# The order of the key-block segments in the value products of a sliding-window attention kernel

## The chip, the cores and the metric

The kernel runs on one core of a Trainium2 chip. The metric is the device time of one execution, in microseconds (us); smaller is better.

## The reference

A layer norm feeds two branches, and their sum is added to the input: a causal attention with a window of 256 tokens (2048 tokens, 32 heads of 16), and a bilinear gated projection.

```python
def _A_ref(x, wqkv, wo):                       # attention; H = 32, Dh = 16, W = 256
    qkv = ...; q, k, v = qkv[0], qkv[1], qkv[2]
    scores = jnp.einsum("bhqd,bhkd->bhqk", q, k) * (Dh ** -0.5)
    mask = (idx[:, None] - idx[None, :] >= 0) & (idx[:, None] - idx[None, :] < W)
    p = _softmax(jnp.where(mask[None, None], scores, -1e9), axis=-1)
    o = jnp.einsum("bhqk,bhkd->bhqd", p, v)    # <- the value products
    return o.transpose(...).reshape(B, S, D) @ wo
def _B_ref(x, w_gate, w_up, w_down):           # (x @ w_gate) * (x @ w_up) @ w_down
    ...
xn = _layernorm(A_x)
return A_x + _A_ref(xn, ...) + _B_ref(xn, ...)
```

## The kernel before

The kernel plans the order of all work itself and keeps TensorE fed with dense products (128 x 128 weights, mostly 512 columns) between the pieces of attention. The tokens are cut into 4 chunks of 512, the heads into 4 sets of 8, which gives 16 value products, here called groups. One group multiplies, for 8 heads at once, the attention strips `P` (keys on the partitions, queries along the columns) with `V`.

A **segment** is one block of 64 keys with the queries that see it: `(k, q, m, at)` is key block `k`, first query block `q`, `m` query blocks (1 to 5) of 64 columns each, and the place `at` in its strip. The first chunk has 9 segments, the others 12:

```python
def layout(T):
    if T == 0:
        return [[(2, 2, 4, 0), (4, 4, 4, 4)], [(0, 0, 5, 0), (5, 5, 3, 5)],
                [(1, 1, 5, 0), (6, 6, 2, 5), (7, 7, 1, 7)], [(3, 3, 5, 0), (2, 6, 1, 5)]]
    return [[(3, 3, 5, 0), (-3, 0, 2, 5), (-4, 0, 1, 7)], [(2, 2, 5, 0), (6, 6, 2, 5), (7, 7, 1, 7)],
            [(0, 0, 5, 0), (5, 5, 3, 5)], [(1, 1, 5, 0), (-2, 0, 3, 5)], [(-1, 0, 4, 0), (4, 4, 4, 4)]]
```

The group takes its segments longest first. Each is 8 matmuls on 8 tiles of the array (2 lanes of 64 rows, 4 strips of 32 columns, of which 17 are used), each with a weight load (LDWEIGHTS) of its own. All segments add into the same two banks, so any order gives the same result but for rounding:

```python
def i_values(self, T, c, strips, banks):
    segments = sorted(((P, s) for P, batch in strips for s in batch), key=lambda x: -x[1][2])
    for n, (P, (k, q, m, at)) in enumerate(segments):
        U, j = divmod(8 * T + k, 8)
        for lane in range(2):
            rows = slice(64 * lane, 64 * lane + 64)
            for e in range(4):
                self.nc.tensor.matmul(
                    banks[lane][32 * e:32 * e + 17, 64 * q:64 * (q + m)],
                    lhsT=self.V[U % 3][rows, j, 4 * c + e, 0:17],
                    rhs=P[rows, e, 64 * at:64 * (at + m)],
                    start=n == 0, stop=n == len(segments) - 1, ...)
```

By length, in blocks, the order is 5,5,5,5,4,4,3,3,2,2,1,1, and 5,5,5,4,4,3,2,1,1 in the first chunk. A group of 12 segments has 96 matmuls ("96-group"; there are 12), one of 9 has 72 ("72-group"; there are 4).

The softmax here doesn't subtract the row's maximum and nothing guards it: scores larger than these inputs give would overflow.

## Time and profile before

| | before |
|---|---|
| time, median of 5 runs | 268.03 us (267.75 to 268.22) |
| PE busy | 260.2 of 265.6 us |
| value products in the chain of waits | 7.4% |
| a 96-group (11 of the 12) / a 72-group, first start to the start of the next product | 1.302 us / 1.047 us |

The head of the page of the kernel before: the span, then busy time and share of each engine. PE is matmul, PEld weight loads.

```profile
span 265.6 us, 7999 instructions
PE 260.2 (98%) x3458; PEld 131.9 (50%) x3458; DVE 189.5 (71%) x365; ACT 165.5 (62%) x122; POOL 119.8 (45%) x272
PEclk9999999999999999999999999999999999999999
```

The two groups of instructions of the value products in the same page: line, engine, operation, tiles, shapes, count, then busy us and mean ns of one, then idle time of the engine just before them.

```profile
L236 PE MATMUL M<-P,V 64*17 64x320 bf16 (+4 forms) x1440 | 20.9, 252 | 0.0
L236 PEld LDWEIGHTS <-V 64*17 64x17 bf16 x1440 | 17.7, 86 | 3.5 <-issue 1.3
```

The chain of waits of the kernel before, in its shares by engine and by line (the view cuts its second line off), and then parts of it in order of time (start us, us, what): a 72-group, and one 96-group between its neighbours.

```profile
PE 95%; DMA 2%; DVE 1%; ACT 0%; issue 0%; DVEq 0%
by line: PE M L204 71.8%; PE S L212 9.4%; PE M L236 7.4%; PE M L664 5.7%; DMA x<-in_A_x_dram 0.9%; DMA out_dram<-xn 0.6%; PE S L204 0.6%; DVE xn L757 0.5%; PE M L603 0.5%; DVE st L577 0.3%; ACT xnT L198 0.2%; issue 0.2%; DVE xn L264 0.2%; A
```

```profile
34.84 1.04 PE M L236 x72
...
112.87 0.65 PE M L204 x3
113.52 0.33 PE S L212 x12
113.85 1.30 PE M L236 x96
115.15 0.01 issue
115.16 1.89 PE M L204 x8
```

PE is the chain. The value products (L236) stand in it with their whole length, no wait of PE stands in front of them, and what they lose or gain shifts everything after. But "busy" hides what goes on inside: PE counts as busy in a group even while it starves (1.30 us busy of the 1.30 us from 113.85 to 115.15 us). The single starts in the trace show that. This is the 96-group that begins at 113.78 us, times in ns from its first start (first and eighth matmul of each segment, first and eighth weight load; worked out from the instruction records):

```
segment blocks   loads         matmuls start   to the next segment
   1      5       -2 ..   21      0 ..   23     141
   2      5       25 ..   48    141 ..  165     136
   ...
   7      3      660 ..  683    767 ..  790      83
   8      3      769 ..  792    850 ..  873      82
   9      2      851 ..  899    932 ..  955      56
  10      2      934 .. 1008    988 .. 1012      56
  11      1     1016 .. 1090   1044 .. 1095      75
  12      1     1099 .. 1173   1119 .. 1177       -
next product                   1301 to 1304 in 11 of the 12 groups, 1375 in this one
```

In this trace a segment of 5, 4, 3 and 2 blocks takes 136, 109, 82.5 and 56 ns to the next one, about 26.7 ns a block; carried on, one of one block should take 29 ns (an estimate from these four). At the end it doesn't: the loads, 3.3 ns apart until then, come 8.3 ns apart from the fourth load of segment 9 on, the first one-block segment takes 75 ns, and the matmuls of the last straggle over 58 ns in place of 23. In this one group the next product really starts 73 ns later than in the others, at 1375 ns: two instructions that only wait for semaphores stand in front of it in the records (at 1157 and 1268 ns), then comes its first load (1344 ns). The chain above shows these 73 ns not as a wait but in the length of the next piece, 1.89 us, since a piece is counted from the end of the one before it.

### The profile page before, as it was taken

How to read it: one execution, taken by the hardware profiler on the slowest of the kernel's cores; microseconds unless marked ns; L12 is line 12 of the kernel's file. 1: busy time of each engine (PE TensorE's matmuls, PEld its weight loads, DVE VectorE, ACT ScalarE, POOL GpSimd, SP SyncE). 2: the span in 40 equal slices, each digit the busy share in tenths (PEclk: the TensorE clock that was granted, in tenths of full speed). 3: DMA queues.
4: the chain of work that ended last, by engine and by line, in shares of the span. 5: the costliest groups of instructions: out<-in, count | busy, mean ns of one | idle time of the engine just before them, and what ended most of it. 6: DMA issues, size and time to landing. Idle time of an engine off the chain costs nothing.

```text
span 265.6 us, 7999 instructions
## 1 busy us (share of the span) xinstructions
PE 260.2 (98%) x3458; PEld 131.9 (50%) x3458; DVE 189.5 (71%) x365; ACT 165.5 (62%) x122; POOL 119.8 (45%) x272
## 2 busy tenths in 40 slices
PE   7999999999999999999999999999999999999994
PEld 6974443654445344464534354456545354544562
DVE  4889987888996629687996629796754449787404
ACT  3637675677677666777667676567886766673000
POOL 1404664554356463708256454718064545537000
PEclk9999999999999999999999999999999999999999
DMA  6999920000001300000001400000000000000002
GB/s 187 373 373 351 225 42 0 4 2 0 4 2 32 89 22 23 0 2 2 2 0 44 81 22 20 0 6 0 2 2 22 21 22 22 0 2 0 2 2 80
DMA packets 17251, 13.88 MB, mean 52 GB/s; under 512 B 7104, under 2 KB 17216, under 8 KB 17216
## 3 DMA queue, kind: packets, MB, share of 16 engines
q1 hardware_dynamic: 16848, 13.11, 17.0%
q8 instruction: 27, 0.44, 0.8%
q10 hardware_dynamic: 368, 0.26, 0.4%
q14 instruction: 8, 0.07, 0.1%
HBM read 9.70 MB, written 2.10 MB: 44 GB/s over the span
## 4 chain that ended last, share of the span: by engine, by line
PE 95%; DMA 2%; DVE 1%; ACT 0%; issue 0%; DVEq 0%
PE M L204 72%; PE S L212 9%; PE M L236 7%; PE M L664 6%; DMA x<-in_A_x_dram 1%; DMA out_dram<-xn 1%; PE S L204 1%; DVE xn L757 1%; PE M L603 0%; DVE st L577 0%; ACT xnT L198 0%; DVE xn L264 0%; ACT ve L581 0%; DVE mv L578 0%; DVE rs L584 0%
## 5 line engine op out<-in xcount | busy, mean ns | idle before, releaser
L488 ACT ACTIVATE P<-S 128x2048 bf16<-128x2048 f32 x76 | 140.9, 1854 | 55.6 <-PE S L212 52.3
L221 POOL TENSOR_SCALAR_AFFINE_SELECT P<-P 64x256 bf16<-64x256 bf16 (+1 forms) x248 | 112.6, 456 | 117.6 <-ACT P L488 104.9
L204 PE MATMUL M<-xnT,Wg 128*128 128x512 bf16 x224 | 57.7, 380 | 0.0
L204 PE MATMUL M<-xnT,Wu 128*128 128x512 bf16 x224 | 57.7, 380 | 0.0
L204 PE MATMUL M<-Wd,hT 128*128 128x512 bf16 (+1 forms) x224 | 52.1, 373 | 0.0
L715 DVE TENSOR_TENSOR hT<-M,gsb 128x512 bf16<-128x512 f32 x56 | 38.2, 682 | 7.7 <-PE M L204 7.4
L204 PEld LDWEIGHTS <-hT 128*128 128x128 bf16 x238 | 21.7, 98 | 23.5 <-issue 2.1
L204 PEld LDWEIGHTS <-Wu 128*128 128x128 bf16 x224 | 20.5, 98 | 25.1 <-issue 2.3
L204 PEld LDWEIGHTS <-Wg 128*128 128x128 bf16 x224 | 20.1, 98 | 24.5 <-issue 2.8
L200 DVE CAST gsb<-M 128x512 bf16<-128x512 f32 x40 | 27.5, 686 | 5.3 <-PE M L204 5.0
L524 DVE STREAM_TRANSPOSE at<-M 128x512 f32<-128x512 f32 x32 | 21.4, 699 | 12.5 <-PE M L236 12.5
L204 PE MATMUL M<-xnT,Wqkv 128*128 128x128 bf16 (+1 forms) x224 | 30.3, 288 | 0.0
L212 PE MATMUL S<-Q,K 32*128 32x320 bf16 (+3 forms) x720 | 30.0, 254 | 0.0
L227 DVE TENSOR_TENSOR P<-P,masks 128x512 int16<-128x512 int16 x56 | 22.7, 412 | 9.2 <-ACT P L488 9.2
L212 PEld LDWEIGHTS <-K 32*128 32x128 bf16 x720 | 11.9, 92 | 32.3 <-issue 31.3
L275 DVE TENSOR_SCALAR K<-M,own 128x512 bf16<-128x512 f32 x28 | 20.0, 742 | 3.4 <-PE M L204 3.2
L204 PEld LDWEIGHTS <-Wqkv 128*128 128x128 bf16 x224 | 15.8, 98 | 10.7 <-issue 1.2
L236 PE MATMUL M<-P,V 64*17 64x320 bf16 (+4 forms) x1440 | 20.9, 252 | 0.0
L236 PEld LDWEIGHTS <-V 64*17 64x17 bf16 x1440 | 17.7, 86 | 3.5 <-issue 1.3
L757 DVE TENSOR_TENSOR y<-M,x 128x512 bf16<-128x512 f32 x12 | 8.2, 682 | 14.8 <-PE M L204 14.8
L204 PE MATMUL M<-Wo,OT 128*128 128x512 bf16 (+1 forms) x64 | 16.2, 374 | 0.0
L664 PE MATMUL M<-Wqkv,xnT 128*64 128x256 bf16 x256 | 15.7, 274 | 0.3 <-ACT xnT L198 0.3
(51 smaller groups left out, 134.1 us busy)
## 6 DMA issues: line engine op xcount, KB each, us to landing
Wg<-in_B_w_gate_dram SPq DMA_DIRECT2D x2, 896.0 KB, 10.1
Wu<-in_B_w_up_dram SPq DMA_DIRECT2D x2, 896.0 KB, 12.1
Wqkv<-in_A_wqkv_dram SPq DMA_DIRECT2D x3, 512.0 KB, 5.4
out_dram<-y SPq DMA_DIRECT2D x12, 128.0 KB, 1.7
x<-in_A_x_dram SPq DMA_DIRECT2D x1, 1024.0 KB, 13.9
Wd<-in_B_w_down_dram SPq DMA_DIRECT2D x2, 512.0 KB, 11.9
Wd<-in_B_w_down_dram SPq DMA_DIRECT2D x2, 384.0 KB, 8.5
x<-in_A_x_dram SPq DMA_DIRECT2D x1, 512.0 KB, 11.4
```

The lines of the kernel that those rows point to most:

```text
L200: self.nc.vector.tensor_copy(out=out, in_=in_)
L204: self.nc.tensor.matmul(ps, lhsT=a, rhs=b, start=first and n == 0, stop=last and n == len(pairs) - 1)
L212: self.nc.tensor.matmul(self.S[:, e, 64 * at:64 * (at + m)], lhsT=self.K[U % 3][rows, c, j].rearrange("p l t -> p (l t)"), rhs=self.Q[T % ...
L221: self.nc.gpsimd.affine_select(out=v, in_=v, pattern=[[0, 4], [0, n], [sign, 64]], base=0, fill=0.0, compare_op=ALU.is_gt if kind else ALU ...
L227: self.nc.vector.tensor_tensor(out=v, in0=v, in1=m, op=ALU.bitwise_and)
L236: self.nc.tensor.matmul(banks[lane][32 * e:32 * e + 17, 64 * q:64 * (q + m)], lhsT=self.V[U % 3][rows, j, 4 * c + e, 0:17], rhs=P[rows, e, ...
L275: self.nc.vector.tensor_scalar(out=out, in0=in_, scalar1=own, scalar2=None, op0=ALU.mult)
L488: ex = self.op(f"exp{g}", {"A": (took + 0.06, took + 0.18)}, [o], lambda e: self.nc.scalar.activation(out=P[:, :, 0:hi], in_=self.S[:, :, ...
L524: t = self.op(f"tr{v}", {"V": (0.63, 0.71)}, [o] + ts, lambda e, par=par: nc.vector.transpose(out=self.at[:, :, par, :], in_=self.M[banks[ ...
L664: self.nc.tensor.matmul(self.M[i][64 * lane:64 * lane + 64, 256 * jj:256 * jj + 256], lhsT=self.xnT[T % 2][:, k, tok], rhs=w[:, lane], sta ...
L715: x = self.op(f"u{T}.{f}", {"V": PSUM_COPY["V"]}, [o, ("gate", T, f)], lambda e: self.nc.vector.tensor_tensor(out=self.hT[T % 2][:, f, :], ...
L757: self.nc.vector.tensor_tensor(out=keep["y"][:, cols], in0=self.M[i][:, cols], in1=self.x[:, t, cols], op=ALU.add)
```

## The change

The intent, from the reading of the end of this group: a short segment gives the next one's weight loads no time to hide, so no two short ones should stand together. Nothing else changes.

```diff
     def i_values(self, T, c, strips, banks):
-        segments = sorted(((P, s) for P, batch in strips for s in batch), key=lambda x: -x[1][2])
+        rest = sorted(((P, s) for P, batch in strips for s in batch), key=lambda x: -x[1][2])
+        segments = []
+        while rest:
+            segments.append(rest.pop(0))
+            if rest:
+                segments.append(rest.pop())
         for n, (P, (k, q, m, at)) in enumerate(segments):
```

The new orders are 5,1,5,1,5,2,5,2,4,3,4,3 and 5,1,5,1,5,2,4,3,4.

## The prediction

> **What bounds the kernel.** TensorE. The page shows PE busy 260.2 of 265.6 us (98%), granted clock full. The chain of waits puts 95% of the span on PE, and 7.4% (19.7 us) on the value products (L236) that the change reorders. There are 16 groups of them, all in the chain, with no wait of PE in front of any: four of 72 matmuls (first chunk, 1.04 us each) and twelve of 96 (1.30 us each). What a group loses or gains is therefore lost or gained by the kernel.
>
> **Inside a group** (starts of single matmuls and weight loads in the trace, group at 113.8 us). A segment is 8 matmuls on 8 tiles of the array, starting 3.3 ns apart. From one segment to the next it takes 136, 109, 82.5 and 56 ns for 5, 4, 3 and 2 blocks of 64 columns[...]; a one-block segment should take 29 ns. But at the end, where the short ones stand together (3,3,2,2,1,1), weight loads no longer come at 3.3 ns: from the third-last segment on they arrive one per 8.3 ns with a gap of 24, about 82.5 ns for 8. The first one-block segment takes 75 ns, and the last one's matmuls straggle over 58 ns in place of 23. The loads for a segment are issued only when the segment before it starts, so a short segment hides few of them. By streaming alone the last start of the 96-group would come at 1068+23 = 1091 ns; it comes at 1177: 86 ns lost. In the 72-group it is 794+23 = 817 against 928: 111 ns lost. After the last start 98 ns plus its columns pass until the next product starts.
>
> **What the change does.** Same 1440 matmuls, same loads, same columns; only the order: 5,1,5,1,5,2,5,2,4,3,4,3 and 5,1,5,1,5,2,4,3,4. The loads behind each short segment then have a long one to hide in. Nothing is added on another engine. A pair 5,1 streams in 165 ns and needs 2 x 82.5 = 165 ns of loads at the starved rate: it just keeps up, and the later pairs (192 ns) have room. The groups should take (estimates from the sums above) 1302 -> about 1220 ns and 1046 -> about 945 ns. Full gain 12 x 0.082 + 4 x 0.10 = 1.4 us. If the starved rate holds already in the early pairs, some 35 to 50 ns of straggling stay in each group, and the gain is about 0.6 us. The strips of the last batch are needed later than before, so no new wait for a mask or an exponential; ACT (62%) and DVE (71%) follow PE.
>
> **Predicted.** 266.9 us, 8 in 10 between 266.3 and 267.9: a gain of about 0.45%. Faster by over 2%: 0.01; within 2%: 0.98; slower by over 2%: 0.01.
>
> **What would show it right.** PE M L236 in the chain falls from 7.4% to about 6.9%; a 96-group takes about 1.22 us to the next product and a 72-group about 0.95; one-block segments take near 29 ns (short of 40); the last segment's matmuls start 3.3 ns apart; all other pieces of the chain keep their lengths.
>
> **What would make it wrong.** Weight loads that can't follow a one-block segment even behind a long one (instruction supply too slow: straggling just moves); a stall when a short product accumulates onto columns just written; a PE wait for a mask newly exposed, since several groups start 50 to 65 ns after a write of an attention strip; or the shifted schedule meeting a PSUM bank not yet free.

No term of the forecast's sum goes with it: the 136, 109, 82.5 and 56 ns are measured, the 29 ns are the estimate above from these four, the streaming sum of the 96-group is 4 x 136 + 2 x 109 + 2 x 82.5 + 2 x 56 + 29 = 1068 ns to its last segment, and the full gain stays 12 x 0.082 + 4 x 0.10 = 1.4 us. That loads are issued with the start of the segment before is read from the table above (first load of segment 8 at 769 ns, first matmul of segment 7 at 767; 851 and 850 for the next).

## The result, and the profile after

The changed kernel takes 267.11 us, median of 5 runs (266.87 to 267.79), against 268.03 us. The ratio is 0.9969, 95% interval 0.9954 to 0.9985. Ratios here and below are the mean time of one kernel's fast runs over that of the other's of the same rounds, so not quite the ratio of the medians quoted. It is the same within 2%, and a little faster, clear of the noise.

The same lines of the page after the change (the line numbers moved by 5).

```profile
span 264.9 us, 7986 instructions
PE 260.4 (98%) x3458; PEld 131.0 (49%) x3458; DVE 190.1 (72%) x365; ACT 165.4 (62%) x122; POOL 119.2 (45%) x272
```

```profile
L241 PE MATMUL M<-P,V 64*17 64x320 bf16 (+4 forms) x1440 | 20.2, 252 | 0.0
...
L241 PEld LDWEIGHTS <-V 64*17 64x17 bf16 x1440 | 15.8, 85 | 2.8 <-issue 1.3
```

The chain of waits after the change, its shares by engine and by line, then the same stretches of it in order of time, and the last group.

```profile
PE 97%; DMA 1%; DVE 1%; ACT 0%; issue 0%
by line: PE M L204 72.0%; PE S L212 9.4%; PE M L241 7.2%; PE M L669 5.7%; PE M L194 1.8%; DMA out_dram<-xn 0.6%; PE S L204 0.6%; DVE xn L762 0.5%; PE M L608 0.5%; ACT xnT L198 0.2%; issue 0.1%
```

```profile
34.93 0.97 PE M L241 x72
...
113.26 0.33 PE S L212 x12
113.59 1.27 PE M L241 x88
114.86 1.83 PE M L204 x8
...
245.99 1.25 PE M L241 x96
```

The matmuls of the group are busy 20.2 in place of 20.9 us, and the 96-group takes 1.27 in place of 1.30 us. (The chain says x88 presumably because some matmuls start out of the program's order: in this group the eighth of segment 6 starts at 548 ns, and three of segment 7 at 528 to 540 ns. All 96 are there.) The piece behind it, 1.83 in place of 1.89 us, no longer holds the 73 ns by which the next product was late before: the same two waiting instructions now come at 997 and 1108 ns, and the product starts at 1270. Over the 16 groups, from the first start to the next product's and without those 73 ns: before 4 x 1.047 + 12 x 1.302 = 19.81 us, after 4 x 0.976 + 11 x 1.270 + 1.249 = 19.12 us, 0.69 us less. From the first start of the first group to the end of the span, the profile falls by 0.77 us (230.85 to 230.08): these 0.69 us and the 73 ns. The spans as a whole differ by 0.7 us, since the first group starts 0.09 us later after the change (34.86 against 34.77 us), and the first 5 us of the two chains run over different work (before, over the load of `x`; after, over the matmuls of L194 that keep TensorE busy at the start). So the gain is all in the value products and in the one product behind them, and that of the groups is half of the 1.4 us that the prediction called the full gain.

Inside the group after the change (the one that begins at 113.52 us; same columns as before):

```
segment blocks   loads         matmuls start
   1      5       -2 ..   22      0 ..   23
   2      1       25 ..   48    142 ..  165
   3      5      143 ..  167    170 ..  193
   4      1      172 ..  195    307 ..  330
   5      5      308, 333, 342 .. 383   335, 339, 346 .. 379, 413
   6      2      418 ..  476    472 ..  548
   ...
  12      3      930 .. 1014   1020, 1025, 1033 .. 1066, 1095
next product                   1270
```

The first half is what the change wanted: the one-block segments take 28 and 28 ns (142 to 170, 307 to 335), not 75. But from segment 5 on the loads come 8.3 ns apart, *behind a short one and behind a long one alike*, and the straggle runs on to the last segment, 75 ns from first to eighth start. One group, the last, ends better: its last segment straggles over 54 ns and it takes 1.249 us.

### The profile page after: what moved, and what is told of

It reads as the page before. It is cut to its first block, busy times and chain, and to the rows that moved or that the text cites. A ratio compares the mean times of both kernels' runs of the same rounds, so it can differ in the third digit from the quotient of the medians.

```text
span 264.9 us, 7986 instructions
## 1 busy us (share of the span) xinstructions
PE 260.4 (98%) x3458; PEld 131.0 (49%) x3458; DVE 190.1 (72%) x365; ACT 165.4 (62%) x122; POOL 119.2 (45%) x272
## 4 chain that ended last, share of the span: by engine, by line
PE 97%; DMA 1%; DVE 1%; ACT 0%; issue 0%
PE M L204 72%; PE S L212 9%; PE M L241 7%; PE M L669 6%; PE M L194 2%; DMA out_dram<-xn 1%; PE S L204 1%; DVE xn L762 1%; PE M L608 0%; ACT xnT L198 0%
## 5 line engine op out<-in xcount | busy, mean ns | idle before, releaser
L221 POOL TENSOR_SCALAR_AFFINE_SELECT P<-P 64x256 bf16<-64x256 bf16 (+1 forms) x248 | 112.2, 455 | 117.4 <-ACT P L493 105.1
L241 PE MATMUL M<-P,V 64*17 64x320 bf16 (+4 forms) x1440 | 20.2, 252 | 0.0
L241 PEld LDWEIGHTS <-V 64*17 64x17 bf16 x1440 | 15.8, 85 | 2.8 <-issue 1.3
```

The costliest lines, as they stand in the source:

```text
L221: self.nc.gpsimd.affine_select(out=v, in_=v, pattern=[[0, 4], [0, n], [sign, 64]], base=0, fill=0.0, compare_op=ALU.is_gt if kind else ALU ...
L241: self.nc.tensor.matmul(banks[lane][32 * e:32 * e + 17, 64 * q:64 * (q + m)], lhsT=self.V[U % 3][rows, j, 4 * c + e, 0:17], rhs=P[rows, e, ...
```

## The experiments

### Two theories

The **neighbour theory** is the prediction's and the change's: the loads of a segment start when the segment before it starts, and hide behind that one. A short one with long neighbours is well placed.

The **queue theory** is the author's reading of the two traces. They show no queue; the word is a picture for what the starts show. In the change the loads of the first 32 pairs of load and matmul, four segments, keep up with the matmuls, and the loads fall behind from the second load of segment 5, pair 34. Suppose that the supply reaches 32 pairs ahead and goes on only when the oldest matmul has *completed*, in program order; then the load of pair p+33 waits for the completion of pair p's matmul. The starts say so, with one constant (completion is start plus duration in the records):

```
kernel   matmul of pair p completes           load of pair p+33 starts                between
after    1st of segment 1:    0 + 302 =  302   2nd load of segment 5:   333            31
before   1st of segment 6:  658 + 269 =  927   2nd load of segment 10:  958            31
before   1st of segment 7:  767 + 243 = 1010   2nd load of segment 11: 1040            30
before   1st of segment 8:  850 + 243 = 1093   2nd load of segment 12: 1123            30
```

(The first load of each of these segments, that of pair p+32, is let in already: it starts early, at 308, 934, 1016 and 1099 ns.) After that the supply gives one pair per 8.3 ns. A long matmul holds its place longer: 302 ns for the first five-block one, 189 ns for a one-block one. By this reading segment k+4 has all its loads in time only if four segments in a row, k to k+3, stream for at least the duration of segment k's matmul plus about 60 ns (31 + 6 x 8.3 + 4 from load to matmul, less the 23 ns by which the eighth start trails anyway). In the change, 5,1,5,1 stream for 136 + 29 + 136 + 29 = 330 ns and would need 302 + 60 = 362.

I worked out the starts of any order from these rules (an estimate from numbers of the two traces: a reach of 32 pairs, 27 ns from a completion to the first instruction let in, which is the 31 ns to the late load less half of 8.3, 8.3 ns a pair, 3.3 ns a pair where the loads keep up, 136, 109, 82.5, 56 and 29 ns a segment of 5 to 1 blocks on each tile, 98 ns plus the last segment's columns, 27 ns a block, to the next product). For the kernel before they give 1.299 us a 96-group, measured 1.302, and 0.998 us a 72-group, measured 1.047; that last difference is told below (two semaphore updates, with which it is about 1.048). Each kernel below is the changed kernel, or where it is said the kernel before, with only the order, or what the diff shows, altered.

### The changed kernel again

No edit; it is timed here on the chip of the next three.

> The changed kernel again, on the same chip as the three other orders. Both theories: groups of 96 take 1.27 us to the next product (1.25 for the last), groups of 72 take 0.976 us; time about 0.7 to 0.8 us under the kernel before (ratio about 0.997).

Measured: correct; 267.09 us against 268.09 us before, ratio 0.9964 (0.9950 to 0.9977). The groups are as before: 1.270 us, and 0.975 to 0.976 us. This repeats the result on another occasion.

### Short one first

```diff
-            segments.append(rest.pop(0))
+            segments.append(rest.pop())
             if rest:
-                segments.append(rest.pop())
+                segments.append(rest.pop(0))
```

> Order 1,5,1,5,2,5,2,5,3,4,3,4 (and 1,5,1,5,2,5,3,4,4): alternation as in the change, but the short one first. Neighbour theory (a segment's loads hide behind the one segment before it; each short one still stands between long ones): as the change, 1.27 and 0.976 us a group. Queue theory [...]: the first segment's matmuls complete after 189 ns in place of 302, so supply for segment 5 resumes early: 1.22 to 1.24 us for a 96-group, 0.945 for a 72-group; 0.4 to 0.5 us faster than the change, ratio to before about 0.995.

Measured: correct; 266.78 us, ratio 0.9951 (0.9935 to 0.9966). Its chain of waits has this for a 96-group:

```profile
113.97 0.33 PE S L212 x12
114.30 1.24 PE M L241 x96
```

1.243 us, 3 ns over the expected range, and 0.949 us for a 72-group. But for the first and the last segment the neighbours are those of the change, so the neighbour theory has no reason for a difference; the queue theory has one, and its size: with a one-block segment in front the first matmul completes at 195 ns, not 302 (the second load of segment 5 starts at 226 ns in place of 333).

### Windows of four that last long enough

```diff
-        while rest:
-            segments.append(rest.pop(0))
-            if rest:
-                segments.append(rest.pop())
+        for m in (5, 3, 3, 5, 1, 4, 5, 1, 5, 4, 2, 2) if T else (4, 5, 1, 3, 5, 2, 4, 5, 1):
+            segments.append(next(x for x in rest if x[1][2] == m))
+            rest.remove(segments[-1])
```

> Order 5,3,3,5,1,4,5,1,5,4,2,2 (and 4,5,1,3,5,2,4,5,1), found with the queue theory so that any four segments in a row last long enough. It ends with two short ones together. Queue theory: no straggle at all, last segment's starts 3.3 ns apart, 1.22 us and 0.943 us a group, ratio to before about 0.9945. Neighbour theory: the closing 2,2 pays about 26 ns and the last one straggles 35 ns, 1.28 us, no better than the change.

Measured: correct; 266.59 us (266.27 to 267.09), ratio 0.9945 (0.9931 to 0.9958), the fastest correct kernel. Its chain and its line in the page:

```profile
113.41 0.33 PE S L212 x12
113.75 1.22 PE M L240 x96
```

```profile
L240 PE MATMUL M<-P,V 64*17 64x320 bf16 (+4 forms) x1440 | 19.5, 252 | 0.0
```

1.218 us a 96-group (1.23 the first; in the third the next product, the one that was late before, comes 48 ns late again) and 0.944 us a 72-group, against 1.22 and 0.943 expected. The last segments start at 991 .. 1014 and 1047 .. 1070 ns: no straggle, with two short ones together at the very end. The sum of the groups is 4 x 0.944 + 12 x 1.218 = 18.39 us, 1.42 us under before. So the full gain that was predicted for the change exists; it takes another order.

### Short ones together, windows as in the change

The edit is as in the last, with the orders 5,5,1,1,5,5,2,2,4,4,3,3 and 5,5,1,1,5,2,4,3,4.

> Order 5,5,1,1,5,5,2,2,4,4,3,3 (and 5,5,1,1,5,2,4,3,4): short ones stand together again, but not at the end. Neighbour theory: each 1,1 costs about 53 ns and the 2,2 about 26 more than in the change, so 1.30 us or more for a 96-group, no gain over before. Queue theory: sums over four segments are those of the change, so 1.25 to 1.275 us and 0.98 us, the same as the change; the two one-block segments run in 29 ns each.

Measured: correct; 267.42 us, ratio 0.9972 (0.9959 to 0.9986). Its chain:

```profile
114.10 1.27 PE M L240 x92
```

96-groups take 1.270 us, as in the change (in one of them the last start is 22 ns later), and 72-groups 0.986 us. The two one-block segments that stand together start at 278, 306 and the next at 335: 28 and 29 ns each. Standing together costs a short segment nothing there; the straggle comes at segment 5, as in the change, whose first four segments have the same sum. The neighbour theory falls.

### Alternating, but late

The orders are 5,5,5,5,3,1,3,1,4,2,4,2 and 5,5,5,3,1,4,1,4,2.

> Order 5,5,5,5,3,1,3,1,4,2,4,2 (and 5,5,5,3,1,4,1,4,2): no two short ones stand together, as the change wants it, but the four longest go first. Neighbour theory: as the change or nearly, 1.27 and 0.98 us a group, ratio about 0.997. Queue theory: the windows of four segments from 3,1,3,1 on are too short (about 225 ns against 243 ns for a three-block matmul to complete, plus the refill), so the loads straggle as before: 1.30 to 1.31 us and about 1.00 to 1.02 us a group, ratio about 0.999 to 1.000.

Measured: correct; 267.55 us, ratio 0.9981 (0.9967 to 0.9996). Its chain:

```profile
113.45 0.33 PE S L212 x12
113.78 1.30 PE M L240 x91
```

1.303 us and 1.003 us. No two short ones stand together, and the 96-groups gain nothing at all over the kernel before. The alternation is thus not what helped.

### Short ones together at the start

```diff
-        segments = sorted(..., key=lambda x: -x[1][2])        (the kernel before)
+        segments = sorted(..., key=lambda x: x[1][2])
```

> Order 1,1,2,2,3,3,4,4,5,5,5,5 (and 1,1,2,3,4,4,5,5,5): the order of before, turned round, short ones together but at the start. Neighbour theory: the opening 1,1 takes about 75 to 82 ns a segment, as it did at the end. Queue theory: [...] the first four run at full speed (29, 29, 56, 56 ns) with loads 3.3 ns apart, and the stall comes at segments 5 to 8; the group takes about 1.305 us (72: 1.004), no gain over before.

Measured: correct; 267.70 us, ratio 0.9973 (0.9959 to 0.9988). Its chain:

```profile
114.66 1.30 PE M L236 x96
```

1.302 us a 96-group, 1.002 us a 72-group, as the queue theory has it. In the trace the first four segments start at 0, 34, 63 and 120 ns: at full speed; these are the first 32 pairs. The fifth, due at 176 ns, starts at 221 and straggles. Its time fell more than its groups explain: 4 x 0.045 = 0.18 us would be a ratio of 0.9993, outside the interval. See below.

### The same lengths, another segment of five first

This one is about what is left over. By the rules above, the change's 96-groups should take 1.252 us, and 11 of 12 take 1.270; only the last takes 1.249. In the eleven, the eighth matmul of segment 5 starts at 413 ns, and in the last at 387. The trace has a semaphore update of PE at 374 ns in each of the eleven (of the semaphore that POOL's masks, L221, wait for) and none in the last group. (Two more, at about 945 and 1005 ns, fall where the last matmuls wait for their tiles: each of segment 12 starts 109 ns after that of segment 11 on its tile, 911 to 1020 and 986 to 1095 ns.) The update belongs to the eighth matmul of the group's first segment, which is key block 3.

```diff
-        rest = sorted(((P, s) for P, batch in strips for s in batch), key=lambda x: -x[1][2])
+        rest = sorted(((P, s) for P, batch in strips for s in batch), key=lambda x: (-x[1][2], x[1][0] == 3))
```

> The change's order of lengths, but among the four five-block segments the one of key block 3 comes last of them, not first. Its last matmul carries the semaphore update that a later mask on POOL waits for. Theory of the update (one holds the supply of instructions for about 25 ns when it is sent): the update moves from 374 ns to about 930 ns after the group's start, the gap of 25 ns before the eighth matmul of segment 5 goes (it starts near 387 in place of 413 ns), and all 96-groups take about 1.25 us, as the last one did; ratio to before about 0.9955. Rival (the gap belongs to the place in the instruction stream, or to the waits in front of segment 5): it stays at 413 ns and 1.27 us, ratio about 0.9965.

Measured: correct; ratio of the fast runs 0.9949 (0.9936 to 0.9963). But the profile fell in a slow execution (299.25 us, clock 0.852) and can't be read against the others. So the kernel ran once more:

> The same kernel as e_tie, since the profile of that run fell in the slow state (clock 0.852) and can't be compared. Theory of the update: no gap at the eighth matmul of segment 5 (start near 387, not 413 ns), 96-groups about 1.25 us, ratio to before 0.995 to 0.996. Rival: 413 ns and 1.27 us, ratio about 0.9965.

Measured: 266.87 us, ratio 0.9955 (0.9930 to 0.9980). The profile is of the fast state:

```profile
113.48 0.33 PE S L212 x12
113.81 1.25 PE M L241 x96
```

The update now comes at 896 ns (about 930 was expected), the eighth matmul of segment 5 starts at 387 ns, and all twelve 96-groups take 1.248 to 1.250 us. After it (896 ns) and after the next update (955 ns) the loads pause, from 905 to 939 and from 964 to 998 ns, 34 ns in place of 8.3 each; the last matmuls, which wait for their tiles, don't feel it. So in these traces one update of a semaphore holds the supply for about 25 ns (34 less 8.3), which costs only where the matmuls are waiting for their loads. The ratio alone, with its interval, would not have told 1.25 from 1.27 us; the trace does.

The same effect fills the gap that the rules left in the 72-groups of the kernel before. There, two updates fall into the starved end of the group, at 830 and 890 ns: the loads pause from 839 to 873 ns, and the last matmuls start at 894 and then 928 ns, 34 ns apart in place of 8.3. (A third, at 755 ns, falls where the next load is held longer anyway, by the completion at 791 ns, to 822 ns.) With twice 25 ns the 0.998 us of the rules become 1.048, and 1.047 were measured. In the changed kernel the next such update comes at 870 ns, after the last start (775 ns). So some 50 of the 71 ns that a 72-group gained come from the place of the updates (an estimate from these numbers), and only some 20 from the straggle that the change was made for. It fits that two orders without any gain in the 96-groups, "alternating late" and "ascending", gain 44 and 45 ns in the 72-groups.

### Half the pairs for the same columns

```diff
-            for lane in range(2):
+            for lane in range(2 if k in (0, 3, 4) else 1):      (on the kernel before; wrong on purpose)
```

> Wrong result on purpose: the order of before, but the second lane is multiplied for key blocks 0, 3 and 4 alone, so most segments have 4 matmuls and 4 loads in place of 8, on the same columns. [...] Queue theory: no starved loads at all, 3.3 ns apart to the end though 2,2,1,1 stand together; one-block segments take 29 ns; 1.204 us and 0.930 us a group. Neighbour theory (a segment's loads start only with the segment before it and come every 8.3 ns with a gap of 24 behind a short one): the closing 1,1 still takes 41 to 57 ns a segment, loads 8.3 ns apart, 1.22 to 1.25 us.

A segment with one lane is 4 pairs, so the 32 pairs of the queue theory are up to eight segments in place of four.

Measured: wrong, as meant; 266.40 us, ratio 0.9932 (0.9918 to 0.9945). Its chain:

```profile
113.24 1.20 PE M L236 x60
```

The groups take 1.205 and 0.930 us, to 1 ns what the queue theory gave, with 2,2,1,1 standing together at the end: loads at 1046, 1050, 1052, 1056, matmuls at 1072 .. 1082. In a 96-group, pairs 34 to 36 in the program's order are still late (loads at 332, 341, 349), just behind the first 32 pairs and the load of the 33rd; the expectation, no starved loads at all, had overlooked them.

### The groups side by side

"Expected" is what the queue theory gave before the run. For the changed kernel it was worked out afterwards, without and with the semaphore updates.

| kernel | 96-group expected | measured | 72-group expected | measured | ratio of time |
|---|---|---|---|---|---|
| changed kernel | 1.252 / 1.275 | 1.270, last 1.249 | 0.977 | 0.976 | 0.9969, 0.9964 |
| short first | 1.22 to 1.24 | 1.243 | 0.945 | 0.949 | 0.9951 |
| windows | 1.22 | 1.218 | 0.943 | 0.944 | 0.9945 |
| pairs | 1.25 to 1.275 | 1.270 | 0.98 | 0.986 | 0.9972 |
| alternating late | 1.30 to 1.31 | 1.303 | 1.00 to 1.02 | 1.003 | 0.9981 |
| ascending | 1.305 | 1.302 | 1.004 | 1.002 | 0.9973 |
| tie | 1.25 | 1.249 | - | 0.975 | 0.9949, 0.9955 |
| one lane | 1.204 | 1.205 | 0.930 | 0.930 | 0.9932 |

**What stays open.** The times fell by somewhat more than the groups in every one of these kernels, by 0.05 us (windows) to 0.5 us (ascending). The traces narrow this down. From the first start of the first group to the end of the span, every profile of another order is shorter than that of the kernel before by what its groups gain, late products such as the one of 73 ns counted, to within 20 ns (ascending 0.26 and 0.26 us, windows 1.44 and 1.42 us; where the record of a next product's first matmul is missing, its start was put 225 ns before the second's). So nothing else was gained in that stretch. What the profiles differ by beyond that lies before the first group, which starts between 34.77 and 35.76 us and which the change of order does not touch. Why the medians of the time all differ in one direction stays open; single fast runs of one kernel lie up to 1.4 us apart, so it may be noise. The verdicts above rest on the groups in the traces, which repeat to a few ns in nearly all groups where no record is missing. Whether the supply goes on at completion, or at some other moment that trails the start by as much, can't be told apart: the ends of matmuls in the profile are modelled, as its reader `prof` says in its help. That this moment grows with the columns, as a completion does, the rows with 302, 269 and 243 ns show.

## Why the prediction was right, and which step of it failed

- *"What a group loses or gains is therefore lost or gained by the kernel."* Right: from the first group on, 0.77 us less in the span, of which 0.69 us in the groups and 73 ns in one product behind a group.
- *The time, 266.9 us in 266.3 to 267.9.* 267.11 us; right, and "within 2%" too. But the middle of the range stood on the full gain, and that did not come; the range holds because it was wide enough for both gains named, 1.4 and 0.6 us (266.6 and 267.4 us). To that extent it is luck.
- *"The groups should take ... 1302 -> about 1220 ns and 1046 -> about 945 ns."* Wrong: 1270 and 976 ns. Gains of 32 and 71 ns, where 82 and 100 were forecast; and of the 111 ns lost in a 72-group, which the prediction put down to loads behind short segments, about 50 were the two semaphore updates.
- *"A pair 5,1 streams in 165 ns and needs 2 x 82.5 = 165 ns of loads at the starved rate: it just keeps up."* This is the step that failed. It takes the supply for a stream that runs on all the time at one pair in 8.3 ns. The traces, read as above, show loads that keep up for 32 pairs and then stand still until the oldest of these matmuls completes: in the change the first matmul completes at 302 ns, and the second load of segment 5 starts at 333. So what counts is not the neighbour but the sum of four segments, against the duration of the first of them.
- *"If the starved rate holds already in the early pairs, some 35 to 50 ns of straggling stay in each group, and the gain is about 0.6 us."* This named the outcome nearly to the number (0.69 us), as the lesser case. The straggle stays from segment 5 to the end.
- *"One-block segments take near 29 ns."* Right, 28 ns. *"The last segment's matmuls start 3.3 ns apart."* Wrong, they straggle over 75 ns. *"Falls from 7.4% to about 6.9%"*, of L236 in the chain: 7.2%, for the same reason; the order from the queue theory has 6.9%.
- Among the dangers named, *"weight loads that can't follow ... (instruction supply too slow: straggling just moves)"* is what happened. There was no stall from adding onto fresh columns (a one-block segment and its follower run at 28 ns) and no new wait of PE in the chain. Not foreseen were the semaphore updates, 20 ns in eleven of the 96-groups after the change.

## What to carry to other kernels

Where many small matmuls run on tiles of the array, count instructions, not only columns. Here, with a load per matmul, the loads reached 32 pairs ahead, and by the reading above a segment has all its loads in time only where the 32 pairs before it stream for longer than the oldest of them takes to complete plus about 60 ns: the change, with 330 ns for 362, straggled and took 1.270 us a 96-group, the windows that last long enough took 1.218. What helped here may be tried there: spread short products so that each such window holds enough columns, and put a short one early in the window (short first: 1.243 us for 1.270). Look at single starts in the trace, since the busy share counted the starved stretches as work (1.30 of 1.30 us). A rule of thumb on neighbours ("no two short ones together") can be met in full and gain nothing (alternating late: 1.303 us for 1.302).
